# Attention into experts: exp's low parts moved from VectorE to GpSimd, with a new plan of times

## The chip, the cores and the metric

The kernel runs on one core of one Trainium2 chip. Its engines work side by side and meet at semaphores: TensorE (PE: matmuls and transposes, results to PSUM; PEld: its weight loads), VectorE (DVE), ScalarE (ACT), GpSimd (POOL, which does not read PSUM here) and SyncE (SP, whose queue issues all DMAs). The metric is device time in microseconds of one launch, as the median of several runs.

## The reference

```python
# q, k, v: (2, 8, 1152, 64) fp32
q_pool = q.reshape(B, H, S // 2, 2, D).mean(axis=3)          # 576 queries a head
scores = scale * q_pool @ k.transpose(0, 1, 3, 2)
attn = exp(scores - scores.max(-1, keepdims=True))
attn = attn / (attn.sum(-1, keepdims=True) + 1e-09)
x = (attn @ v) -> (1152, 512)
for e in range(4):                                            # w1 (4,512,1024), w2 (4,1024,512)
    out += p[:, e:e+1] * (relu(x @ w1[e]) @ w2[e])
a, b = out @ mw1, out @ mw2                                   # float64 weights
return ((a * b) @ w3) @ w_out
```

## The kernel before

Sixteen heads are worked in eight pairs (i = 0 to 7; s = 0, 1 is the head in the pair). To keep fp32's accuracy on fast matmuls, an operand is cut in a high part and a low part (value minus high part), and products of parts are summed.

For a pair, K is transposed on TensorE into bank tiles (`kt`, line 269) in two groups, six transposes and three; ScalarE copies the high part `kab` (line 272), VectorE the low part `kl` (line 275). GpSimd adds neighbouring queries (`pool_q`, lines 240 and 243), TensorE transposes them (`qt`, line 323), ScalarE writes the high part `qh` and rows 0 to 63 of QZ (lines 332, 333), VectorE the low part `ql` (line 326), and GpSimd rows 64 to 127 of QZ (line 329) in pieces of 512 and 64 columns. Row maxima come from cheaper matmuls (`mp`, line 381), five blocks for head 0 and four for head 1, each a two-bank and a one-bank tile (tags `w0`, `w1`, one buffer each) that VectorE reduces (`mx`, line 384). The maxima of a head (`mf`) are transposed (`mr`, line 416, also `w1`), cut (`mh` on ScalarE, `ml` on VectorE, line 424) and laid into Q2 by four small DMAs (`place`). DMAs (`plan_spread`) lay the parts of K and Q into K1, K2, Q1, Q2.

A head's scores come in nine chunks of 128 keys (`s`, line 535: four matmuls into one of two double banks). ScalarE writes the exp in fp32 (`pf`, line 545). Its upper 16 bits are the high part `pht`; the low part `plt` is `pf` minus that. GpSimd makes it (line 556) for chunks not in `LO_DVE`; for chunk 2 of head 0 and chunks 5 and 7 of head 1 ScalarE makes the exp a second time in the bank (`again`, line 549) and VectorE subtracts from there (line 554), so that the bank is held until then. V's parts are `v_hi` (line 510, ScalarE) and `v_lo` (line 514, VectorE). The attention product (`av`, lines 577 and 579) takes 135 small matmuls a head, ordered by five query blocks, then nine chunks, then three products; its first 27 therefore read all nine chunks. It is spread over the following half, with one accumulator bank, and `out_of` normalises it on VectorE (lines 583 to 595, `x` and `XT`).

All of this is written as an agenda: each step is entered with a time by `at(t, f)`, where one unit is about one chunk, and the steps are emitted in the order of their times. Nothing waits for a time: it only sets each engine's order of instructions. A pair has 18 units. The constants at the file's head are those times: `EX` to exp, `LO` and `LOV` to the low parts, `KT`, `KH`, `KL_` for K, `QT`, `QH_`, `QL_` for Q, `MX0`, `MX1` for maxima, `TURNS` for `mr`, `mh`, `ml` and `place`, `AV0`, `AVN` and `AVW` for start, length and density of the attention product.

The first expert's start is woven into the last pair: its weights (`WT`), the scale of x (`plan_rows`: `cm`, `cxt`, `ca`, `cxs`, `cx`, at `CX`), four transposes of x (`XA`, `XS`, `XC`, line 775 and lines 789, 794) which use a pool of three banks (`one_bank`) together with the spread of the weight maxima (`ws`, line 656, whose `bounds` run on VectorE at lines 445 to 449), two hidden tiles in four pieces each (`UA`, `US`) and two output tiles (`DT`, `DS`).

Of the kernel before, what the change touches and what calls it, by code (L numbers as in the profile page):

```python
# [9 lines left out]

TURN = 1.03
TURNS = (1.03, 1.23, 1.43, 1.93)
TURN0 = (0.05, 0.45, 0.55, 0.65)
KH = 0.79
KL_ = 0.32
QH_ = 0.05
QL_ = 1.2
M0 = 0.35
M1 = 0.01
M2 = 0.49  # L20
LO_DVE = ((2,), (5, 7))
EX = 0.44
EX2 = 0.6
LO = 0.9
LOV = 0.82
AV0 = 1.14
AVN = 7.68
AVW = ((0.8, 0.1, 0.85, 0.28, 1.25, 0.44, 0.55, 2.95), (1.0, 1.5, 0.42, 2.08, 1.5, 0.5, 0.62, 1.25))
VH = 0.35
VL = 2.06  # L30
VL0 = -5.21
VR = 5.67
VE = 0.9
V1 = (5.5, 1.4)
VL1 = 7.8
QZ1 = 0.25
VLZ = 2.7
K0 = 1.2
Q0 = 0.51
L0 = (5.7, 5.8)  # L40
LV2 = 15.6
PQ = 2.57
PQS = 0.3
SH = -5.85
XR = 136.9
CX = 128
CXT = (0, 0.3, 0.35, 1.2, 1.25)
LK1 = -10
LQ1 = -10
# [9 lines left out]
FIRST = (0.71, 1.14, 2.3, 3.1)  # L59
NEAR = 0.0  # L60
LATER = 0
KT = (3.05, 3.05)
QT = 4.84
MX0 = (7.0, 8.1, 9.9, 11.82, 13.01)
MXF = (7.3, 8.3, 10, 11.72, 13.01)
MX1 = (14, 16, 17.2, 18.92)
ME = -0.03
SW = 130
W1 = 134
WT = ((123.5, 129.6, 130.6, 132.7, 138.5, 133.3, 133.5, 135.6, 135.8), (2, 8.5))  # L70
WN = (1, 4, 5, 3, 0)
WN2 = (1, 4, 4, 3, 0)
WS = 6
XA = 0.2
XS = 1.1
XC = (0.75, 1.1)
UA = 136.6
US = 2
DT = (140.6, 143.8)
OUT = 0.1  # L80
XB = 147
DS = 1.1
TICKS = ((), (), (), (0, 1), (), (2,), (0, 4, 13), (2, 9), (), (0, 2, 10), (2, 8, 9), (14,), (0, 10), (2,), (2, 6, 14), (2, 4, 7), (0, 1))
FT = ((7,), (5,), (3,), (4,), (7,), (3,), (), (4,))
GT = ((0, 2), (2,), (0, 1, 2), (0, 2), (0, 1), (0, 1), (), (0,))
# [1 line left out]
W3T = 7  # L87
MX = 7
STAGED = 4
EV = 1  # L90

F32 = mybir.dt.float32
F32R = mybir.dt.float32r
# [18 lines left out]
def tile_kernel(ctx: ExitStack, tc: tile.TileContext, q, k, v, dp, w1, w2, mw1, mw2, mw3, mwo, out):  # L112
    nc = tc.nc
# [11 lines left out]
    NPAIR = B * H // 2  # L125
# [9 lines left out]
    f32 = lambda ap: ap.bitcast(F32)  # L135
# [55 lines left out]
    QZ = k_p.tile([P, 2 * T], F32R, name="QZ")  # L191
# [7 lines left out]
    KAB, KL, QH, QL = {}, {}, {}, {}  # L199
# [32 lines left out]
    def at(t, f, *args):  # L232
        agenda.append((t, len(agenda), f, args))
# [18 lines left out]
    def plan_k(i, t):  # L252
# [7 lines left out]
        for g in range(2):  # L260
# [54 lines left out]
    def plan_q(i, t, tv):  # L315
        st = {}

        def pe():
            QH[i] = kq_p.tile([P, T], F32R, tag="qh", name=f"qh{i}")
            QL[i] = kq_p.tile([P, T], F32R, tag="ql", bufs=1, name=f"ql{i}")  # L320
            ps = st[0] = work(0, f"qt{i}").rearrange("p n c -> p (n c)")
            for j in range(NB + 1):
                nc.tensor.transpose(ps[:, j * P : (j + 1) * P], QP[:, j], ident)  # L323

        def lo():
            nc.vector.tensor_tensor(out=QL[i], in0=st[0][:, :T], in1=f32(QH[i]), op=ALU.subtract)

        def one(lo, hi, to):
            nc.gpsimd.tensor_copy(QZ[64:128, to : to + hi - lo], f32(QH[i][64:128, lo:hi]))

        at(t, pe)
        at(tv, lambda: nc.scalar.copy(out=QH[i], in_=st[0][:, :T]))
        at(tv + 0.02, lambda: nc.scalar.copy(out=QZ[0:64, :T], in_=st[0][0:64, :T]))
        at(tv + QL_, lo)
        tz = tv + (QZ1 if i == 1 else 0.6)
        at(tz, one, 0, NB * P, T + TL)
        at(tz, one, NB * P, T, T)

# [20 lines left out]
    def plan_max(i, s, times):  # L359
# [29 lines left out]
        for t, j in zip(times, blocks):  # L389
            at(t + NEAR, pe, j, 0)  # L390
            at(t + M0, reduce, j, 0)
            at(t + (M1 if i == 0 else 2 * NEAR), pe, j, 1)
# [128 lines left out]
    def plan_scores(i, s, t):  # L521
        for c in range(NC):
            st = {}

            def pe(c=c, st=st):
                if c == 0:
                    if i + s:
                        pft[i, s] = ph_p.tile([P, NC, T], F32, tag="pf", name=f"pf{i}_{s}")
                    pht[i, s] = pft[i, s].bitcast(BF16).rearrange("p c (t w) -> p c t w", w=2)[:, :, :, 1]
                    plt[i, s] = ph_p.tile([P, NC, T], F16, tag="pl", name=f"pl{i}_{s}")  # L530
                ps = st["s"] = ps_s.tile([P, 2, 512], F32, tag="s", name=f"s{i}_{s}_{c}")
                cs = slice(c * P, (c + 1) * P)
                for a, b, first in ((K1, Q1, True), (K2, Q2, False)):
                    for n in range(2):
                        mm(  # L535
                            ps[:, n, :HALF], a[s][:, cs], b[s][:, n * HALF : (n + 1) * HALF],
                            start=first, stop=not first,
                        )

            two = lambda ap: ap.rearrange("p (n t) -> p n t", n=2)  # L540

            on_dve = c in LO_DVE[s]

            def whole(c=c, st=st):
                nc.scalar.activation(out=two(pft[i, s][:, c, :]), in_=st["s"][:, :, :HALF], func=AF.Exp, scale=SCORE)  # L545

            def again(c=c, st=st):
                x = st["s"][:, :, :HALF]
                nc.scalar.activation(out=x, in_=x, func=AF.Exp, scale=SCORE)

            def lo(c=c, st=st, on_dve=on_dve):
                o, f, h = plt[i, s][:, c, :], pft[i, s][:, c, :], pht[i, s][:, c, :]
                if on_dve:
                    nc.vector.tensor_tensor(out=two(o), in0=st["s"][:, :, :HALF], in1=two(h), op=ALU.subtract)  # L554
                else:
                    nc.gpsimd.tensor_tensor(out=o, in0=f, in1=h, op=ALU.subtract)  # L556

            at(t + c, pe)
            at(t + c + EX, whole)
            if on_dve:  # L560
                at(t + c + EX2, again)
            at(t + c + (LOV if on_dve else LO), lo)

    def plan_av(i, s, t, span):
        b, h = PAIRS[i]
        xd = slice((h + s) * D, (h + s + 1) * D)
        xo = X[b][:, :, xd]
        st = {}

        def one(j, c, n):  # L570
            if (j, c, n) == (0, 0, 0):
                st["t"] = ps_a.tile([P, NB + 1, D + 1], F32, tag="a", name=f"av{i}_{s}")
            o = j * P if j < NB else T - P
            p = (pht, pht, plt)[n][i, s][:, c, o : o + P]
            t = st["t"]
            if n == 1:
                mm(t[:, j, 0:D], p, vt[s][:, c, 0:D], start=False, stop=False)  # L577
            else:
                mm(t[:, j, :], p, vt[s][:, c, D:], start=(c == 0 and n == 0), stop=(c == NC - 1 and n == 2))  # L579

        def out_of():
            dn = tiny.tile([P, NB + 1], F32, tag="dn", name=f"dn{i}_{s}")
            nc.vector.tensor_scalar(
                out=dn, in0=st["t"][:, :, D], scalar1=PS * EPS, scalar2=vs[i][:, s : s + 1],
                op0=ALU.add, op1=ALU.mult,
            )
            nc.vector.reciprocal(out=dn, in_=dn)
            n = NB if b else NB + 1
            nc.vector.tensor_tensor(
                out=xo[:, :n], in0=st["t"][:, :n, :D], in1=dn[:, :n].unsqueeze(2).to_broadcast([P, n, D]), op=ALU.mult  # L590
            )
            if b:
                r = slice(64, 128)
                nc.vector.tensor_scalar(  # L594
                    out=XT[r, xd], in0=st["t"][r, NB, :D], scalar1=dn[r, NB:], scalar2=None, op0=ALU.mult
                )

        todo = [(j, c, n) for j in range(NB + 1) for c in range(NC) for n in range(3)]

        share = AVW[s] if span == AVN else (1,) * 8  # L600
        ends = [sum(share[:n]) / sum(share) for n in range(9)]
        for k, x in enumerate(todo):
            y = k / len(todo)
            n = max(m for m in range(8) if ends[m] <= y)
            at(t + span * (n + (y - ends[n]) / (ends[n + 1] - ends[n])) / 8, one, *x)
        at(t + span + OUT, out_of)


# [240 lines left out]
    with tc.manual_schedule():  # L849
# [15 lines left out]
        for b in range(B):  # L865
            nc.sync.dma_start(
                out=pr_raw[:, b * NB : (b + 1) * NB, :],
                in_=dp[b * T : b * T + NB * P].rearrange("(p j) e -> p j e", j=NB),
# [33 lines left out]
        for i in range(NPAIR):  # L902
            nx = i + 1 < NPAIR
            t = 18 * i
# [8 lines left out]
            if nx:  # L913
# [3 lines left out]
                u = t + (LATER if i == 0 else 0)  # L917
# [110 lines left out]
    with tc.manual_schedule():  # L1028
# [182 lines left out]
        for t, (pe, add) in enumerate(down_tiles(last_task, bank)):  # L1211
# [10 lines left out]
            if t in (4, 6, 8):  # L1222
                lo, hi = {4: (0, 4), 6: (4, 6), 8: (6, 9)}[t]
# [115 lines left out]
```

## Time and profile before

| | us |
|---|---|
| runs | 823.51, 821.10, 821.26; median 821.26 |
| profiled execution | 819.96 |
| its span, first to last instruction | 818.2 |
| PE busy | 797.2 (97%) |
| DVE busy | 609.6 (75%) |
| ACT busy | 405.1 (50%) |
| POOL busy | 274.3 (34%), nearly all before 260 us |

Attention is the first third of the span. In times shown as 121.77 the span's start is zero. A matmul's record is longer than its share of TensorE, because matmuls overlap: the step from one start to the next is what TensorE spends.

### The profile page before, as it was taken

How to read it: one execution, taken by the hardware profiler on the slowest of the kernel's cores; microseconds unless marked ns; L12 is line 12 of the kernel's file. 1: busy time of each engine (PE TensorE's matmuls, PEld its weight loads, DVE VectorE, ACT ScalarE, POOL GpSimd, SP SyncE). 2: the span in 40 equal slices, each digit the busy share in tenths (PEclk: the TensorE clock that was granted, in tenths of full speed). 3: DMA queues.
4: the chain of work that ended last, by engine and by line, in shares of the span. 5: the costliest groups of instructions: out<-in, count | busy, mean ns of one | idle time of the engine just before them, and what ended most of it. 6: DMA issues, size and time to landing. Idle time of an engine off the chain costs nothing.

```text
span 818.2 us, 15685 instructions
## 1 busy us (share of the span) xinstructions
PE 797.2 (97%) x6301; PEld 523.9 (64%) x6301; DVE 609.6 (75%) x1086; ACT 405.1 (50%) x735; POOL 274.3 (34%) x264
## 2 busy tenths in 40 slices
PE   8799999999999999999999999999999999999998
PEld 7688888888877555555555555555554446556787
DVE  6888889888885666779978999988788877772000
ACT  2565666566573543334445466636564545553111
POOL 5667766676661000001101124303331323442100
PEclk9999999999999999999999999999999999999999
DMA  8866756684630121123323332321357752300011
GB/s 185 219 142 165 186 135 151 154 182 105 162 80 2 52 103 52 52 78 103 108 74 103 104 103 78 103 77 52 80 143 139 176 127 75 97 3 1 14 52 51
DMA packets 85976, 83.28 MB, mean 102 GB/s; under 512 B 49624, under 2 KB 67408, under 8 KB 85904
## 3 DMA queue, kind: packets, MB, share of 16 engines
q1 hardware_dynamic: 85904, 82.29, 38.9%
q8 instruction: 49, 0.80, 0.4%
q14 instruction: 23, 0.19, 0.1%
HBM read 51.92 MB, written 2.36 MB: 66 GB/s over the span
## 4 chain that ended last, share of the span: by engine, by line
PE 86%; DVE 9%; DMA 2%; issue 1%; ACT 1%; SPq 1%; POOL 0%; DVEq 0%; ACTq 0%; POOLq 0%
PE up L705 23%; PE dn L745 22%; PE gt L1277 11%; PE s L535 7%; PE o L1293 6%; PE wf L1246 5%; PE mp L381 4%; PE av L579 4%; DVE mx L384 4%; PE av L577 2%; DVE pl L554 1%; DMA rk<-in_k 1%; DVE vt L514 1%; DMA rw<-in_moe_w 1%; PE qt L323 1%
## 5 line engine op out<-in xcount | busy, mean ns | idle before, releaser
L745 PE MATMUL dn<-w,h 128*128 128x512 f16 x840 | 183.9, 379 | 0.0
L556 POOL TENSOR_TENSOR pl<-pf 128x576 f16<-128x576 f32 x120 | 140.4, 1186 | 67.8 <-ACT pf L545 67.7
L705 PEld LDWEIGHTS <-w 128*128 128x128 f16 x1152 | 111.6, 98 | 76.0 <-DVE w L676 0.8
L745 PEld LDWEIGHTS <-h 128*128 128x128 f16 x840 | 81.5, 98 | 95.7
L545 ACT ACTIVATE pf<-s 128x576 f32<-128x576 f32 x144 | 93.2, 649 | 55.9 <-PE s L535 55.4
L535 PE MATMUL s<-Q,K 128*128 128x288 f32 x576 | 110.4, 314 | 2.9 <-ACT pf L545 1.7
L384 DVE TENSOR_REDUCE mx<-mp 128x1 f32<-128x768 f32 (+1 forms) x144 | 101.8, 751 | 13.4 <-PE mp L381 11.9
L705 PE MATMUL up<-xB,w 128*128 128x320 f16 x768 | 109.9, 299 | 0.5 <-DVE xB L794 0.5
L844 POOL TENSOR_TENSOR wo<-wo,cv_a 128x512 f32<-128x512 f32 x20 | 25.8, 1293 | 226.6 <-DVE wo L841 128.8
L711 ACT ACTIVATE up<-up 128x320 f32<-128x320 f32 (+1 forms) x96 | 45.8, 477 | 112.9 <-PE up L705 91.7
L705 PE MATMUL up<-xA,w 128*128 128x512 f16 x384 | 89.0, 379 | 0.3 <-DVE w L676 0.3
L535 PEld LDWEIGHTS s<-Q,K 128*128 128x128 f32 x576 | 83.9, 191 | 4.9 <-ACT pf L545 2.1
L579 PE MATMUL av<-vt,pf 128*128 128x65 f16 x720 | 83.1, 194 | 1.6 <-DVE XT L594 1.5
L579 PE MATMUL av<-vt,pl 128*128 128x65 f16 x720 | 83.2, 195 | 0.0
L577 PE MATMUL av<-vt,pf 128*128 128x64 f16 x720 | 82.2, 193 | 0.0
L716 DVE TENSOR_TENSOR h<-up,h 128x320 f16<-128x320 f32 (+1 forms) x94 | 50.1, 550 | 42.9 <-ACT h L712 42.5
L1277 PEld LDWEIGHTS <-mw 128*128 128x128 f16 x576 | 55.9, 98 | 36.8
L579 PEld LDWEIGHTS <-pf 128*128 128x128 bf16 x720 | 66.9, 99 | 8.3 <-DVE XT L594 2.8
L579 PEld LDWEIGHTS <-pl 128*128 128x128 f16 x720 | 67.0, 97 | 4.6 <-issue 1.1
L577 PEld LDWEIGHTS <-pf 128*128 128x128 bf16 x720 | 67.1, 98 | 3.9 <-issue 1.1
L381 PE MATMUL mp<-kab,QZ 128*128 128x384 f32 x216 | 57.8, 374 | 1.3 <-DVE mx L384 1.0
L759 DVE SCALAR_TENSOR_TENSOR x2B<-dn,sh,x2B 128x512 f32<-128x512 f32 x75 | 52.9, 743 | 4.7 <-PE dn L745 4.0
(183 smaller groups left out, 1200.4 us busy)
## 6 DMA issues: line engine op xcount, KB each, us to landing
rw<-in_moe_w SPq DMA_DIRECT2D x64, 512.0 KB
K<-kab SPq DMA_DIRECT2D x32, 288.0 KB
rk<-in_k SPq DMA_DIRECT2D x16, 288.0 KB
rv<-in_v SPq DMA_DIRECT2D x8, 576.0 KB
Q<-qh SPq DMA_DIRECT2D x32, 144.0 KB
K<-kl SPq DMA_DIRECT2D x16, 288.0 KB
rq<-in_q SPq DMA_DIRECT2D x8, 512.0 KB
rw<-in_moe_w_out SPq DMA_DIRECT2D x8, 512.0 KB
```

The lines of the kernel that those rows point to most:

```text
L381: mm(ps[:, n, :PC], QZ[:, o : o + P], KAB[i][:, sl], start=True, stop=True)
L384: nc.vector.tensor_reduce(out=mx[i, s][:, j, g : g + 1], in_=st.pop((j, g))[:, :, :PC], axis=AX.XY, op=ALU.max)
L535: mm(ps[:, n, :HALF], a[s][:, cs], b[s][:, n * HALF : (n + 1) * HALF], start=first, stop=not first,)
L545: nc.scalar.activation(out=two(pft[i, s][:, c, :]), in_=st["s"][:, :, :HALF], func=AF.Exp, scale=SCORE)
L556: nc.gpsimd.tensor_tensor(out=o, in0=f, in1=h, op=ALU.subtract)
L577: mm(t[:, j, 0:D], p, vt[s][:, c, 0:D], start=False, stop=False)
L579: mm(t[:, j, :], p, vt[s][:, c, D:], start=(c == 0 and n == 0), stop=(c == NC - 1 and n == 2))
L705: mm(p, w[:, a, c, fc * P : (fc + 1) * P], x[b][:, c, lo - o : hi - o], start=(c == 0 and a == b), stop=(c == KD - 1 and a == 1),)
L716: nc.vector.tensor_tensor(out=hl[:, fc, lo:hi], in0=st["p"], in1=hh[:, fc, lo:hi], op=ALU.subtract)
L745: mm(p, hid[n][a][:, fc, t * P : (t + 1) * P], w[:, b, fc, :], start=(fc == 0 and a == b), stop=(fc == 1 and a == 1),)
L759: nc.vector.scalar_tensor_tensor(out=acc, in0=st["p"], scalar=share, in1=acc, op0=ALU.mult, op1=ALU.add)
L1277: mm(p, mws[n][:, a, m * KD + c], x[:, b * KD + c, lo - o : hi - o], start=(c == 0 and a == b), stop=(c == KD - 1 and a == 1),)
```

## The change

`LO_DVE` becomes empty, so in pairs 0 to 6 GpSimd makes all eighteen low parts; in the last pair `LASTD` names chunk 4 of head 0 and chunks 0 and 7 of head 1 for VectorE. The upper 512 columns of QZ's lower half are copied by ScalarE from PSUM. Chunks get times of their own (`SPOS`, not in pair 0), the attention matmuls' times are rounded up to steps of 0.02 (`AVS`), and most other times are new.

```diff
-TURNS = (1.03, 1.23, 1.43, 1.93)
+TURNS = (1.08, 1.18, 2.08, 2.53)
-KH = 0.79
-KL_ = 0.32
-QH_ = 0.05
-QL_ = 1.2
-M0 = 0.35
+KH = 0.49
+KL_ = 0.62
+QH_ = 1.1
+QL_ = 0.25
+M0 = 0.4
-LO_DVE = ((2,), (5, 7))
-EX = 0.44
-EX2 = 0.6
-LO = 0.9
-LOV = 0.82
-AV0 = 1.14
-AVN = 7.68
-AVW = ((0.8, 0.1, 0.85, 0.28, 1.25, 0.44, 0.55, 2.95), (1.0, 1.5, 0.42, 2.08, 1.5, 0.5, 0.62, 1.25))
-VH = 0.35
-VL = 2.06
-VL0 = -5.21
-VR = 5.67
-VE = 0.9
+LO_DVE = ((), ())
+LASTD = ((4,), (0, 7))
+LOL = 0.85
+EX = 0.79
+EX2 = 0.85
+LO = 2.45
+LOV = 1.15
+AV0 = 1.49
+AVN = 7.48
+AVW = ((0.64, 0.05, 1.06, 0.45, 1.0, 0.14, 0.2, 2.36), (0.8, 1.47, 1.71, 2.49, 0.72, 0.32, 0.55, 1.54))
+VH = 0.8
+VL = 2.36
+VL0 = -5.71
+VR = 4.82
+VE = 0.2
...
-PQ = 2.57
-PQS = 0.3
+PQ = 0.52
+PQS = 0.65
-XR = 136.9
-CX = 128
+XR = 138.35
+CX = 128.8
-KT = (3.05, 3.05)
-QT = 4.84
-MX0 = (7.0, 8.1, 9.9, 11.82, 13.01)
+KT = (3.05, 3.5)
+QT = 4.54
+MX0 = (7.0, 8.1, 9.35, 12.27, 13.06)
+SPOS = ((0, 0.8, 2.1, 3, 4.4, 5, 6.2, 7, 7.9), (0.1, 1, 2.1, 3, 4, 5, 6, 7, 7.65))
+AVS = 0.02
+AVP = 2.35
-MX1 = (14, 16, 17.2, 18.92)
-ME = -0.03
-SW = 130
-W1 = 134
+MX1 = (14.0, 16.2, 17.25, 18.82)
+ME = 0.12
+SW = 130.8
+W1 = 133.8
...
-XA = 0.2
-XS = 1.1
-XC = (0.75, 1.1)
-UA = 136.6
-US = 2
-DT = (140.6, 143.8)
-OUT = 0.1
+XA = 0.35
+XS = 0.55
+XC = (0.9, 1.1)
+UA = 135.5
+US = 2.1
+DT = (140.8, 144.1)
+OUT = 0.35
...
         def one(lo, hi, to):
-            nc.gpsimd.tensor_copy(QZ[64:128, to : to + hi - lo], f32(QH[i][64:128, lo:hi]))
+            if lo:
+                nc.gpsimd.tensor_copy(QZ[64:128, to : to + hi - lo], f32(QH[i][64:128, lo:hi]))
+            else:
+                nc.scalar.copy(out=QZ[64:128, to : to + hi - lo], in_=st[0][64:128, lo:hi])
...
-            on_dve = c in LO_DVE[s]
+            on_dve = c in (LO_DVE[s] if i < NPAIR - 1 else LASTD[s])
...
-            at(t + c, pe)
-            at(t + c + EX, whole)
+            u = t + (SPOS[s][c] if i else c)
+            at(u, pe)
+            at(u + EX, whole)
             if on_dve:
-                at(t + c + EX2, again)
-            at(t + c + (LOV if on_dve else LO), lo)
+                at(u + EX2, again)
+            at(u + (LOV if on_dve else LO if i < NPAIR - 1 else LOL), lo)
...
-            at(t + span * (n + (y - ends[n]) / (ends[n + 1] - ends[n])) / 8, one, *x)
+            u = t + span * (n + (y - ends[n]) / (ends[n + 1] - ends[n])) / 8
+            if span == AVN:
+                u = math.ceil((u - AVP) / AVS) * AVS + AVP
+            at(u, one, *x)
```

## Rows read from the trace of the kernel before

**Rows 1.** Page: the chain that ended last, share of the span by engine.
```profile
PE 86%; DVE 9%; DMA 2%; issue 1%; ACT 1%; SPq 1%; POOL 0%; DVEq 0%; ACTq 0%; POOLq 0%
```
**Rows 2.** Stretches: length, busy time of PE, PEld, DVE, ACT, POOL, clock, DMA share, GB/s.
```profile
18.80:32.79 13.99, 9.82 (x56) 7.44 (x56) 11.17 (x23) 7.64 (x15) 7.05 (x9) 1.00 0.87 204
32.79:36.20 3.41, 3.34 (x12) 3.23 (x13) 2.80 (x6) 1.27 (x4) 3.25 (x3) 0.50 1.11 298
121.77:150.16 28.39, 27.55 (x392) 24.33 (x389) 24.81 (x42) 17.36 (x29) 20.01 (x21) 1.00 0.68 158
```
**Rows 3.** Waits of weight loads, 36.63 to 221.2: who for whom, us, times, longest.
```profile
PEld mp L381 <- DVE mx L384: 5.9, 32, 0.3
PEld kt L269 <- DVE ml L424: 5.8, 6, 1.0
...
PEld s L535 <- DVE pl L554: 1.7, 7, 0.2
```
**Rows 4.** VectorE in order of time, 138 to 142.9: start, us, instruction.
```profile
138.75 2.12 DVE L514 SCALAR_TENSOR_TENSOR vt<-rv,vs,vt 128x576 f16<-128x576 f32 x1
140.79 0.74 DVE L554 TENSOR_TENSOR pl<-s,pf 128x576 f16<-128x576 f32 x1
141.46 0.27 DVE L424 TENSOR_TENSOR ml<-mr,mh 5x128 f32<-5x128 f32 x1
```
**Rows 5.** Groups of ScalarE, 121.77 to 150.16: busy us, mean ns, idle before.
```profile
L549 ACT ACTIVATE s<-s 128x576 f32<-128x576 f32 x3 | 1.9, 647 | 0.0
...
L333 ACT CAST QZ<-qt 64x576 fp32r<-64x576 f32 x1 | 0.6, 631 | 0.0
```
**Rows 6.** Groups of GpSimd, 121.77 to 150.16.
```profile
L556 POOL TENSOR_TENSOR pl<-pf 128x576 f16<-128x576 f32 x16 | 18.6, 1178 | 8.1 <-ACT pf L545 8.1
```
**Rows 7.** Order of time, 120 to 165, matmuls.
```profile
121.72 0.19 PE L577 MATMUL av<-vt,pf 128*128 128x64 f16 x1
121.75 0.19 PE L579 MATMUL av<-vt,pl 128*128 128x65 f16 x1
...
121.77 0.79 PE L535 MATMUL s<-Q,K 128*128 128x288 f32 x4
...
123.00 0.69 PE L535 MATMUL s<-Q,K 128*128 128x288 f32 x4
```
**Rows 8.** Order of time, 133.5 to 136.3: last `place` DMA, next pair's first chunk.
```profile
133.63 0.53 SPq L430 DMA_DIRECT2D Q<-ml  x1
...
136.00 0.51 PE L535 MATMUL s<-Q,K 128*128 128x288 f32 x2
```
**Rows 9.** VectorE in order of time, 228 to 236.
```profile
229.32 0.80 DVE L514 SCALAR_TENSOR_TENSOR vt<-rv,vs,vt 128x576 f16<-128x576 f32 x1
...
232.36 1.03 DVE L448 TENSOR_SCALAR wab<-wab 128x2 f32<-128x2 f32 x1
...
233.50 0.73 DVE L794 SCALAR_TENSOR_TENSOR xA<-xt,cx,xA 128x512 f16<-128x512 f32 x1
```
**Rows 10.** Line 556, whole span: ns shortest, median, longest.
```profile
L556 POOL TENSOR_TENSOR pl<-pf x120: 1139/1147/2104, 24.3 to 252.4; 128x576 f16<-128x576 f32 x120
```
**Rows 11.** Waits of matmuls, 25 to 33.5.
```profile
PE mr L416 <- DVE mf L401: 1.4, 1, 1.4
PE qt L323 <- DVE kl L275: 1.0, 1, 1.0
PE s L535 <- ACT pf L545: 0.7, 1, 0.7
PE vp L461 <- DVE vm L457: 0.4, 1, 0.4
```
**Rows 12.** Waits of matmuls, 221.2 to 262.
```profile
PE av L579 <- DVE XT L594: 1.3, 2, 0.7
PE s L535 <- ACT pf L545: 1.0, 2, 0.6
PE s L535 <- DVE cx L497: 0.4, 1, 0.4
PE cxt L482 <- DVE cm L476: 0.3, 1, 0.3
```

More of the change, by code (lines that the diff above doesn't have):

```diff
@@ L11 @@
 TURN = 1.03
-TURNS = (1.03, 1.23, 1.43, 1.93)
+TURNS = (1.08, 1.18, 2.08, 2.53)
 TURN0 = (0.05, 0.45, 0.55, 0.65)
-KH = 0.79
-KL_ = 0.32
-QH_ = 0.05
-QL_ = 1.2
-M0 = 0.35
+KH = 0.49
[3 more added lines that the diff above has]
+M0 = 0.4
 M1 = 0.01
 M2 = 0.49
-LO_DVE = ((2,), (5, 7))
-EX = 0.44
-EX2 = 0.6
-LO = 0.9
-LOV = 0.82
-AV0 = 1.14
-AVN = 7.68
-AVW = ((0.8, 0.1, 0.85, 0.28, 1.25, 0.44, 0.55, 2.95), (1.0, 1.5, 0.42, 2.08, 1.5, 0.5, 0.62, 1.25))
-VH = 0.35
-VL = 2.06
-VL0 = -5.21
-VR = 5.67
-VE = 0.9
+LO_DVE = ((), ())
[13 more added lines that the diff above has]
+VE = 0.2
 V1 = (5.5, 1.4)
 VL1 = 7.8
-QZ1 = 0.25
-VLZ = 2.7
+QZ0 = 0.25
+QZ1 = 0.1
+VLZ = 2.55
 K0 = 1.2
@@ L61 @@
 LATER = 0
-KT = (3.05, 3.05)
-QT = 4.84
-MX0 = (7.0, 8.1, 9.9, 11.82, 13.01)
-MXF = (7.3, 8.3, 10, 11.72, 13.01)
-MX1 = (14, 16, 17.2, 18.92)
-ME = -0.03
-SW = 130
-W1 = 134
-WT = ((123.5, 129.6, 130.6, 132.7, 138.5, 133.3, 133.5, 135.6, 135.8), (2, 8.5))
+KT = (3.05, 3.5)
[4 more added lines that the diff above has]
+AVP = 2.35
+MXF = (7.3, 8.3, 10, 11.72, 13.01)
+MX1 = (14.0, 16.2, 17.25, 18.82)
+ME = 0.12
+SW = 130.8
+W1 = 133.8
+WT = ((123.5, 129.6, 130.6, 132.7, 138.5, 133.3, 133.5, 135.6, 135.8), (2, 8.8))
 WN = (1, 4, 5, 3, 0)
@@ L73 @@
 WS = 6
-XA = 0.2
-XS = 1.1
-XC = (0.75, 1.1)
-UA = 136.6
-US = 2
-DT = (140.6, 143.8)
-OUT = 0.1
-XB = 147
-DS = 1.1
+XA = 0.35
[5 more added lines that the diff above has]
+OUT = 0.35
+XB = 148.6
+DS = 1.3
 TICKS = ((), (), (), (0, 1), (), (2,), (0, 4, 13), (2, 9), (), (0, 2, 10), (2, 8, 9), (14,), (0, 10), (2,), (2, 6, 14), (2, 4, 7), (0, 1))
@@ L89 @@
 STAGED = 4
-EV = 1
+EV = 1.3
 F32 = mybir.dt.float32
@@ L334, in plan_q @@
         at(tv + QL_, lo)
-        tz = tv + (QZ1 if i == 1 else 0.6)
+        tz = tv + (QZ0 if i == 1 else QZ1)
         at(tz, one, 0, NB * P, T + TL)
```

## The prediction

> **What bounds the kernel now.** I read the chain of waits first. TensorE carries 86% of it and VectorE 9% [rows 1], so a microsecond is won only where TensorE stands still. The change touches the attention stage and its seam to the experts, up to about 262 us; what follows has the same work in the same order. So I took the busy time of stretches. One pair of heads lasts 28.39 us (121.77 to 150.16) with VectorE busy 24.81, ScalarE 17.36 and GpSimd 20.01 [rows 2]: no helper is full, but VectorE at 87% is late at places. The stretch 32.79 to 36.20 stands out: TensorE was granted half its clock there, after 13.99 us in which it was busy only 9.82 [rows 2].
>
> Then TensorE's waits. From 36.63 to 221.2 its weight loads waited 5.9 us in 32 waits for a row maximum, 5.8 us in 6 waits (0.97 each) on line 269 for `ml`, and 1.7 us in 7 waits on line 535 for the VectorE subtraction of line 554 [rows 3]. The 0.97 comes once a pair: the second group of K transposes needs the bank that the turned maxima `mr` still hold until `ml` has read it. On VectorE `ml` stood behind 2.12 us of `vt` (line 514) and 0.74 of line 554 [rows 4].
>
> **The change part by part.** *Low parts to GpSimd.* In seven pairs three chunks each lose a second exp (0.647 on ScalarE [rows 5]) and a VectorE subtraction (0.74 [rows 4]) and get a GpSimd subtraction (1.178 [rows 6]). Per pair ScalarE loses 1.9, VectorE 2.2, and GpSimd gains 3.5. The upper 512 columns of QZ go from GpSimd to ScalarE; that copy is not in the trace, and lies between zero and the 0.631 of the 576-column copy beside it [rows 5]; I take 0.6, the nearest row. GpSimd then has 20.0 + 3.5 - 0.6 = 22.9 us of a pair of about 27.5, ScalarE 16.1, VectorE 22.6. The extra copy sits ahead of one exp; the score chunk that needs this exp's bank comes two chunks and some 24 attention matmuls later, about 2 x 0.7 + 24 x 0.03 = 2.1 us [rows 7], against 0.6 + 0.65. I cost it at nothing; without that cover it is 0.6 in 7 pairs, 4.2 us.
>
> *What this takes off TensorE.* The 1.7 us of waits for line 554 go: the bank is now free after one exp. The K transposes are helped twice: 0.74 is gone ahead of `ml`, and the second group is asked for 0.45 plan units later with ten attention matmuls in between, 0.3 us. 0.74 + 0.3 covers the 0.97, but `mr` moves behind a score chunk and `vt` stays directly ahead, so I leave 0.2: 6 x 0.77 = 4.6 us gained (bounds: nothing, 5.8). For the maxima I take 1.0 of the 5.9 (0 to 5.9): their spacing changes both ways, and a wait of 0.18 is partly the weight load that could not run ahead.
>
> *What is added on TensorE.* A score chunk directly behind attention matmuls takes 0.79, behind a maxima matmul 0.69 [rows 7]: a switch costs 0.10. Laid out by their times, a pair has 24 such switches where it had 21: 3 x 7 x 0.10 = 2.1 at most; two of the three stand before short transposes, and I take 1.5. Middle pairs: -4.6 - 1.7 - 1.0 + 1.5 = -5.8 us.
>
> *Moved steps with no cost.* `place` (four DMAs) comes half a plan unit later in the SP queue, past nothing but its own wait; K and Q loads swap. The last of the four `ml`/`mh` DMAs is issued at 133.63 and takes 0.53, and the next pair's first chunk, their reader, starts at 136.00 [rows 8]: 1.8 us of cover for issue and landing, of which the change takes about 0.3. The Q pooling on GpSimd goes behind two low parts (2.4 us), with about 5 us until its transpose. The vector `vp` matmul is asked for one chunk earlier than the reduction behind it may be done; it waited 0.4 for that in the first pair [rows 11], so 0 to 0.4 a pair; I take 0, since `ml` and `kl` ahead of it start earlier too.
>
> *Port.* Line 514 shows two lengths, 0.80 [rows 9] and 2.12 [rows 4], and a GpSimd low part of 1.147 median reached 2.104 [rows 10]. The 2.12 stand in the middle pairs, where line 514 meets GpSimd at work already, so I add nothing. [...]
>
> *First pair.* In it TensorE waits 1.4 us for `mf`, 1.0 for `kl` and 0.7 for an exp [rows 11]. `mf` comes 0.75 earlier without line 554. The first K transposes now come before `mr`, so they run inside that wait; `kl` for six transposes is asked separately, ahead of the reduction. The exp that held a bank no longer stands behind the Q copies. I take 1.8 of the 3.1. The half clock I leave in; if it went, 3.41 us would become 1.7.
>
> *Last pair and first expert tiles.* TensorE's waits there: 1.3 for `XT` (the normalised output), 1.0 for exp, 0.4 and 0.3 around the scale chain `cx`, `cm`, 3.0 together [rows 12]. In the new order an expert piece stands between chunks 0 and 1 of the second head, both down pieces stand ahead of the last attention head, and `cxt` comes behind `mr`: all four waits should go. New ones come. The spread `cxs` follows `cxt` after 23 matmuls (0.7 us) while its chain has five small VectorE operations, each at most about the 0.27 of `ml` [rows 4], 1.35 in all: 0 to 0.65, and I take 0.4. And the fourth x transpose follows the weight spread `ws` at once; it needs the bank of the second, whose VectorE half stands behind the weight scales: 1.03 for the slowest of these and 0.73 for the half itself [rows 9]. That is between 0.73 and about 2.2; I take 1.8. Net -3.0 + 0.4 + 1.8 = -0.8 us.
>
> **Sum.** -5.8 - 1.8 - 0.8 = -8.4 us. The profiled execution took 819.96 us, a span of 818.2 and 1.76 around it; it becomes 811.6. The median of three runs is 821.26, 1.3 above the profiled one; from it the forecast is 812.9.
>
> **Rivals.**
> B, the port gives the gain back. Each of two `vt` operations a pair stays at 2.12 or grows by one more low part (1.15), `ml` is late again and the K wait stays: the 4.6 and the 1.0 are lost, and middle pairs are -1.7 + 1.5 = -0.2. With the first and last pair at half of my figures, -1.3: 819.8. For it: line 514 was 2.12 where GpSimd worked without a break, and GpSimd will do so more. Against: line 554 is gone from that queue in any case.
>
> C, slower: GpSimd becomes the bound. The attention matmuls read all nine low parts of a head in their first 27, so a late one stops TensorE. GpSimd's 22.9 us leave 5.5 of a pair of 28.39, 0.305 for each of 18 low parts: it decides once their mean passes 1.178 + 0.305 = 1.48 us, which lies between the median and the longest [rows 10]. At 1.53 a pair lasts 18 x 0.05 = 0.9 longer: 7 x 0.9 = 6.3 us, 827.6. Against: two collisions a pair of the longest kind, 0.96 each, add only 0.11 to the mean.
>
> D, the seam eats more. The new waits at `cxs` and the fourth transpose take 0.4 + 2.2, the low part of chunk 4 on VectorE holds the bank of chunk 6 for its 0.74, a third of the old 3.0 comes back, and TensorE's clock falls as it fell after the waits of the first pair: 3.41 us at half clock, 1.7 lost. The seam is then -3.0 + 2.6 + 0.7 + 1.0 + 1.7 = +3.0 in place of -0.8: 816.7.
>
> E, the stage is freed further: maxima waits halve (2.0 more), and the half clock of the first pair goes (1.7): 809.2.
>
> **How the numbers follow.** Chances: forecast 0.46, E 0.14, D 0.13, B 0.16, C 0.11. A measurement tells 0.3% (2.5 us) from no change. The forecast, E and D are faster; B is mostly the same, split 0.03, 0.10, 0.03; C slower 0.10, same 0.01. Together faster 0.76, same 0.11, slower 0.13. The forecast's own range is 809 to 817; 8 in 10 reach from 806 (E with all K waits gone) to 821.5 (B with a new wait of 0.25 a pair), leaving C and a little of B and E out.
>
> **What would show it.** Pairs of about 27.5 us in place of 28.39, and no wait of line 269 above 0.3 each; no line 554 before 200 us, and 22 to 23.5 us of GpSimd a pair; a transpose of the fourth x block that waits 1 to 2 us for VectorE; the half-clock stretch still near 33 us. It is wrong if attention matmuls wait for `pl`, if line 514 has a mean over 2.1, or if a middle pair is longer than 28.2 us.

## The result, and the profile after

The changed kernel takes 813.03 us (median of 4 runs, 812.85 to 813.24) against 821.64 of the kernel before beside it: 0.9891 of its time, with an interval of 0.9874 to 0.9908. The forecast was 812.9. The profiled execution took 812.85 us with a span of 811.1, which is 7.1 less than the 819.96 and 818.2 of before.

TensorE's work did not get smaller (6301 matmuls in both kernels), it waits less. From the page, the chain that ended last, by engine [rows 1]:

```profile
PE 86%; DVE 10%; DMA 1%; ACT 1%; issue 1%; SPq 0%; ACTq 0%
```

Busy time of stretches: length, PE, PEld, DVE, ACT, POOL, clock, DMA share, GB/s [rows 2]. The second is where TensorE ran at half clock before; the third is one pair of heads.

```profile
18.97:32.80 13.83, 10.59 (x60) 8.01 (x60) 11.23 (x25) 7.14 (x14) 7.82 (x10) 1.00 0.91 202
32.80:36.20 3.40, 2.95 (x16) 2.34 (x17) 2.58 (x4) 2.07 (x5) 3.40 (x4) 1.00 0.97 238
132.74:160.35 27.61, 27.40 (x393) 24.43 (x389) 22.39 (x39) 16.06 (x27) 23.27 (x23) 1.00 0.72 162
```

A pair lasts 27.61 us in place of 28.39, with TensorE busy all but 0.21 of it. GpSimd has 23.27 us and VectorE 22.39 (22.9 and 22.6 were expected), and the half clock is gone in this execution.

Waits of weight loads from 35.47 to 215.5, all groups [rows 3]:

```profile
PEld mp L390 <- DVE mx L393: 4.2, 19, 1.1
PEld L589 <- issue: 2.2, 14, 0.2
PEld mp L390 <- DVE ql L332: 2.2, 6, 0.4
PEld L587 <- issue: 1.9, 12, 0.2
PEld L589 <- DVE XT L604: 0.5, 2, 0.3
```

The 5.8 us of the K transposes for `ml` and the 1.7 for the old VectorE subtraction have no row any more, the maxima fell from 5.9 to 4.2, and a new row has come: maxima matmuls wait 0.37 a pair for `ql`. Why the first went is seen on VectorE and GpSimd in order of time (start, us, instruction) [rows 4]:

```profile
135.96 0.15 DVE L410 TENSOR_REDUCE mf<-mx 128x1 f32<-128x2 f32 x1
136.03 0.81 DVE L523 SCALAR_TENSOR_TENSOR vt<-rv,vs,vt 128x576 f16<-128x576 f32 x1
137.06 0.28 DVE L433 TENSOR_TENSOR ml<-mr,mh 5x128 f32<-5x128 f32 x1 [0.22 <-ACT mh L429]
...
141.66 1.04 DVE L457 TENSOR_SCALAR vs<-vs 128x2 f32<-128x2 f32 x1
142.74 0.17 DVE L458 RECIPROCAL vs<-vs 128x2 f32<-128x2 f32 x1
142.85 0.76 DVE L332 TENSOR_TENSOR ql<-qt,qh 128x576 fp32r<-128x576 f32 x1
```
```profile
134.33 1.15 POOL L565 TENSOR_TENSOR pl<-pf 128x576 f16<-128x576 f32 x1 [1.44 <-ACT pf L554]
135.44 1.98 POOL L246 TENSOR_TENSOR QP<-rq 128x256 f32<-128x256 f32 x2
137.39 1.14 POOL L565 TENSOR_TENSOR pl<-pf 128x576 f16<-128x576 f32 x1
...
141.54 2.38 POOL L565 TENSOR_TENSOR pl<-pf 128x576 f16<-128x576 f32 x2
```

`vt` took 0.81 us here where it took 2.12: it came in between the two pooling adds of line 246, and `ml` now waits for ScalarE, not for `vt`. The new wait for `ql` starts at line 457: two columns of four bytes took 1.04 us, because a low part had begun on GpSimd 0.12 earlier (shown below, one column at a time). With GpSimd idle, at 19.2, the same operation took 0.17.

Low parts on GpSimd in that pair [rows 6] and the new copy on ScalarE (busy us, mean ns, idle before):

```profile
L565 POOL TENSOR_TENSOR pl<-pf 128x576 f16<-128x576 f32 x19 | 21.9, 1174 | 4.3 <-ACT pf L554 4.1
```
```profile
L338 ACT CAST QZ<-qt 64x512 fp32r<-64x512 f32 x1 | 0.6, 583 | 0.0
```

Waits of matmuls in the first pair, 18.97 to 35.47 [rows 11]:

```profile
PE mp L390 <- DVE mx L393: 1.0, 4, 0.4
PE mp L390 <- ACT QZ L338: 1.0, 1, 1.0
PE kt L275 <- DVE ml L433: 0.7, 1, 0.7
PE qt L329 <- DVE kl L281: 0.4, 1, 0.4
PE vp L470 <- DVE kl L281: 0.4, 1, 0.4
PE kt L275 <- DVE mx L393: 0.2, 1, 0.2
```

And from 215.5 to 262, the seam to the experts [rows 12]:

```profile
PE cxs L503 <- DVE cxd L497: 1.3, 1, 1.3
PE up L718 <- DVE xB L807: 0.5, 1, 0.5
PE xt L788 <- DVE xB L807: 0.3, 1, 0.3
PE xt L788 <- DVE wab L454: 0.2, 1, 0.2
```

A half of a pair begins with its first score chunk. Measured from one such start to the next, in the profiled executions of this case:

| kernel | first pair | half with K transposes | other half | median us | ratio to before |
|---|---|---|---|---|---|
| before | 17.85 + 14.19 | 14.17 | 14.23 | 821.3 to 822.0 | 1 |
| changed | 16.50 + 14.49 | 13.95 | 13.63 | 813.03 | 0.9891 [0.9874, 0.9908] |
| new plan, old low parts | 16.70 + 14.92 | 13.96 | 14.09 | 817.42 | 0.9942 [0.993, 0.9954] |
| before, low parts alone | 17.00 + 14.47 | 17.2 (15.7 once) | 13.93 | 834.85 | 1.0159 [1.014, 1.0177] |
| before, pooling alone | 17.30 + 14.77 | 13.75 | 14.23 | 819.33 | 0.9969 [0.9959, 0.9979] |
| before, low parts and pooling | 16.78 + 14.48 | 13.36 | 13.94 | 814.63 | 0.9925 [0.99, 0.995] |
| changed, old pooling | 16.53 + 14.50 | 15.06 | 13.64 | 821.01 | 1.0001 [0.9989, 1.0012] |
| changed, one column | 16.42 + 14.46 | 13.56 | 13.62 | 810.73 | 0.9861 [0.9848, 0.9875] |
| one column, QZ from SBUF | 15.94 + 13.90 | 13.60 | 13.62 | 809.49 | 0.9857 [0.9842, 0.9871] |
| one column, QZ on GpSimd | 15.82 + 14.50 | 13.38 | 13.63 | 808.28 | 0.9834 [0.982, 0.9848] |

Of the 7.1 us, twelve middle halves have 4.8, the first pair and its start 0.9, and the last pair with all that follows 1.4. That last figure has two parts: the last attention matmul starts 2.1 us sooner after the start of its half (21.68 in place of 23.83), and 0.7 is lost again far behind, in expert work that the change does not touch. From the 401st to the 801st matmul of the output tiles (line 758) the changed kernel takes 169.1 us, the kernel before 168.4, and the others of the table 169.0 to 170.3.

### The profile page after: what moved, and what is told of

Read it like the earlier page. It is cut to its first block, busy times and chain, and to the rows that moved or that the text cites. A ratio compares the mean times of both kernels' runs of the same rounds, so it can differ in the third digit from the quotient of the medians.

```text
span 811.1 us, 15625 instructions
## 1 busy us (share of the span) xinstructions
PE 794.8 (98%) x6301; PEld 522.8 (64%) x6301; DVE 593.3 (73%) x1065; ACT 396.0 (49%) x722; POOL 295.7 (36%) x277
## 4 chain that ended last, share of the span: by engine, by line
PE 86%; DVE 10%; DMA 1%; ACT 1%; issue 1%; SPq 0%; ACTq 0%
PE dn L758 21%; PE up L718 21%; PE gt L1290 12%; PE s L544 8%; PE o L1306 6%; PE wf L1259 5%; PE av L589 5%; PE mp L390 5%; DVE mx L393 3%; PE av L587 2%; DVE vt L523 1%; PE kt L275 1%; DVE vs L457 1%; DVE ql L332 1%; DMA rk<-in_k 1%; DMA rw<-in_moe_w 1%
## 5 line engine op out<-in xcount | busy, mean ns | idle before, releaser
L565 POOL TENSOR_TENSOR pl<-pf 128x576 f16<-128x576 f32 x141 | 162.7, 1175 | 48.7 <-ACT pf L554 47.5
L589 PE MATMUL av<-vt,pf 128*128 128x65 f16 x720 | 85.0, 194 | 0.1
L544 PEld LDWEIGHTS s<-Q,K 128*128 128x128 f32 x576 | 82.0, 189 | 2.4 <-issue 0.6
```

The lines of the kernel that those rows point to most:

```text
L544: mm(ps[:, n, :HALF], a[s][:, cs], b[s][:, n * HALF : (n + 1) * HALF], start=first, stop=not first,)
```

## The experiments

**The new plan without the moved low parts.** The changed kernel with the old choice of chunks in pairs 0 to 6.

```diff
-LO_DVE = ((), ())
+LO_DVE = ((2,), (5, 7))
```


> The new plan of times with the old share of low parts (chunk 2 of head 0, chunks 5 and 7 of head 1 again on VectorE with a second exp, pairs 0 to 6). Theory 1, the gain comes from work taken off VectorE and off the score banks: the 0.74 us ahead of the cut maxima and the bank waits come back, 5 to 7 us slower than the changed kernel, near 818 to 820. Theory 2, the gain comes from the order (K transposes in two steps, expert pieces between chunks): within 2 us of the changed kernel, 813 to 815.

817.42 us, between the ranges of the two theories. By the ratios the plan alone is worth 4.8 of a gain of 9.0, the moved low parts under it the other 4.2. They show where VectorE used to subtract from the bank in head 1: 14.09 against 13.63. The halves with K transposes take 13.96 here as in the changed kernel, and the weight loads of the K transposes wait 0.3 us in all from 36.17 to 217, although a subtraction again stands ahead of `ml`:

```profile
138.51 0.81 DVE L523 SCALAR_TENSOR_TENSOR vt<-rv,vs,vt 128x576 f16<-128x576 f32 x1
139.25 0.76 DVE L563 TENSOR_TENSOR pl<-s,pf 128x576 f16<-128x576 f32 x1
139.93 0.27 DVE L433 TENSOR_TENSOR ml<-mr,mh 5x128 f32<-5x128 f32 x1
```

So in the new plan that wait went without the moved low parts, with `vt` at 0.81.

**The moved low parts without the new plan.**

```diff
-            on_dve = c in LO_DVE[s]
+            on_dve = i == NPAIR - 1 and c in LO_DVE[s]
```


> The old plan of times with all low parts of pairs 0 to 6 on GpSimd, and nothing else. Theory 1: most of the gain of the middle pairs and half of that of the first pair without a new plan: waits of line 269 for the cut maxima fall from 0.97 to about 0.2 and the waits for line 554 go; 4 to 7 us faster than before, 815 to 818. Theory 2: less than 2 us faster, 820 to 822, because the old times put something else in the way.

834.85 us: 13 slower. The part that I took for the source of the gain costs more, alone, than the whole change brings. The waits of weight loads from 36 to 235, then VectorE and GpSimd at one of the places:

```profile
PEld kt L269 <- DVE ml L424: 15.1, 6, 2.5
```
```profile
84.87 0.15 DVE L401 TENSOR_REDUCE mf<-mx 128x1 f32<-128x2 f32 x1
84.93 4.32 DVE L514 SCALAR_TENSOR_TENSOR vt<-rv,vs,vt 128x576 f16<-128x576 f32 x1
89.18 0.27 DVE L424 TENSOR_TENSOR ml<-mr,mh 5x128 f32<-5x128 f32 x1
```
```profile
84.87 0.45 POOL L243 TENSOR_TENSOR QP<-rq 64x128 f32<-64x128 f32 x1
85.29 3.35 POOL L556 TENSOR_TENSOR pl<-pf 128x576 f16<-128x576 f32 x3
```

`vt` began 0.06 us behind a pooling add and ended 0.61 after the last of three low parts that GpSimd ran directly behind it: 4.32 us for an operation that took 0.81 in the changed kernel. Both its inputs (`rv`, `vt`) lie in SBUF, as GpSimd's do. `ml` stands behind it, and the K transposes wait for `ml`. This is rival B's mechanism at twice the size that I gave it: 2.2 us more than the 2.12 of before, where I priced 1.15. Where a K wait was that long, TensorE was granted half its clock for 3.41 us behind it in five of the six pairs of the profiled execution, as in the first row here; the mean clock of the pair around it was 0.95 (columns of rows 2):

```profile
89.56:92.97 3.41, 3.41 (x37) 3.20 (x38) 2.57 (x3) 1.13 (x2) 0.31 (x1) 0.50 0.17 37
84.90:116.00 31.10, 28.83 (x388) 25.68 (x386) 24.89 (x39) 15.79 (x26) 23.24 (x24) 0.95 0.62 143
```

Wait and clock together are the 3.1 us by which those halves grew: the wait is 2.5 in place of 0.97, and the one half that kept its clock is 1.5 shorter (15.7). The trace shows that `vt` was kept out through four instructions of GpSimd (3.70 us), and not by what.

So which other edit of the change keeps `vt` out of this? The candidate was the Q pooling, whose add stood ahead of those low parts.

**Before, with the low parts and the pooling's new times.** To the edit above:

```diff
-PQ = 2.57
-PQS = 0.3
+PQ = 0.52
+PQS = 0.65
```


> The kernel before, with GpSimd making all low parts of pairs 0 to 6, and with one more thing of the change: the Q pooling on GpSimd at its new times (PQ 0.52, PQS 0.65). Theory (the 13 us lost by the low parts alone are VectorE's vt, which is kept out of work as long as GpSimd runs instructions one directly behind the other, and the pooling adds are what made GpSimd late there): the 64-row pooling add no longer stands ahead of three waiting low parts, vt drops from up to 4.33 us to below 2.2, the halves with K transposes go from about 17.2 us back to 14.4 or less, total 814 to 820. Rival 1 (the low parts overload GpSimd under the old times wherever the pooling stands): vt stays above 3 us once a pair, total 830 to 836. Rival 2 (the K transposes' times, not vt, make the wait): vt short, but the wait of the K transposes for ml stays above 1 us a pair, total 821 to 829.

814.63 us. Two constants took back 19 us (by the ratios). `vt` at the same place, and GpSimd:

```profile
80.62 1.71 DVE L514 SCALAR_TENSOR_TENSOR vt<-rv,vs,vt 128x576 f16<-128x576 f32 x1
82.25 0.27 DVE L424 TENSOR_TENSOR ml<-mr,mh 5x128 f32<-5x128 f32 x1
```
```profile
79.46 2.25 POOL L556 TENSOR_TENSOR pl<-pf 128x576 f16<-128x576 f32 x2 [1.59 <-ACT pf L545]
81.67 1.24 POOL L240 TENSOR_TENSOR QP<-rq 128x256 f32<-128x256 f32 x1
82.88 1.14 POOL L556 TENSOR_TENSOR pl<-pf 128x576 f16<-128x576 f32 x1
```

`vt` now meets one low part and gets in ahead of the pooling add, which is the one that waits (1.24 us; with the low parts alone two of these adds took 1.43 together, at 82.13). The wait of the K transposes is gone, and the halves with them, 13.36 us, are shorter than in the changed kernel. The theory's figure for `vt` (below 2.2) and total held; both rivals fell.

**The changed kernel with the pooling's old times.** The same edit the other way round.

> The changed kernel with the Q pooling on GpSimd back at its old times (PQ 2.57, PQS 0.3) and nothing else. Theory (the pooling's place decides whether vt meets an unbroken run of GpSimd): vt above 2 us in middle pairs again, ml and the K transposes late, halves with K transposes above 14.5 us in place of 13.95, total 818 to 832. Rival (the new plan of turns and K transposes has enough room, and the pooling's time matters little): vt may be long, but TensorE does not wait for it, total 812 to 815.

821.01 us: the whole gain is gone. Waits of weight loads from 36 to 220, and `vt` beside GpSimd:

```profile
PEld kt L275 <- DVE ml L433: 7.5, 6, 1.3
```
```profile
81.87 2.60 DVE L523 SCALAR_TENSOR_TENSOR vt<-rv,vs,vt 128x576 f16<-128x576 f32 x1
84.40 0.27 DVE L433 TENSOR_TENSOR ml<-mr,mh 5x128 f32<-5x128 f32 x1
```
```profile
80.50 3.35 POOL L565 TENSOR_TENSOR pl<-pf 128x576 f16<-128x576 f32 x3
84.69 1.15 POOL L565 TENSOR_TENSOR pl<-pf 128x576 f16<-128x576 f32 x1 [0.84 <-ACT pf L554]
```

**The pooling's new times alone, in the kernel before.**

> The kernel before with the Q pooling on GpSimd at its new times (PQ 0.52, PQS 0.65) and nothing else: what the move of the pooling is worth without the low parts. Theory (two separate terms: the pooling shortens only the run of GpSimd that vt meets, and the low parts take their subtraction of 0.74 out of VectorE's queue ahead of ml): vt in the halves with K transposes 1.7 to 1.8 instead of 2.12, the wait of the K transposes for ml 0.5 to 0.7 instead of 0.97, total 818 to 820.5. Rival 1 (the pooling's place was the whole gain of the kernel with low parts and pooling, 7 us): 813.5 to 816. Rival 2 (without the low parts the pooling's time does nothing): 821 to 822.5.

819.33 us, the theory's range. `vt` fell from 2.12 to 1.70 and the wait of the K transposes from 5.8 to 3.3 us in 6. With it the four corners are there: pooling alone -2.6, low parts alone +13, both -6.2 (all by their ratios). The moved low parts are worth -3.6 behind a moved pooling and +13 without it.

What `vt` took follows in each kernel from what GpSimd ran, by the records of both near the same place of a pair:

| kernel | GpSimd while `vt` stood there | ends after `vt`'s start | `vt` us |
|---|---|---|---|
| before | add, low part | 1.50 | 2.12 |
| pooling alone; low parts and pooling | rest of a low part | 1.09 | 1.71 |
| low parts alone | add, three low parts | 3.70 | 4.32 |
| changed, old pooling | rest of a low part, low part | 1.99 | 2.60 |
| changed | rest of an add | 0.14 | 0.81 |

In each row `vt` ends 0.61 to 0.67 us after the GpSimd instruction that kept it out.

**The bounds and `cxd` one column at a time.** The same arithmetic in more and smaller operations.

```diff
-        nc.vector.tensor_scalar(out=up, in0=up, scalar1=top, scalar2=low, op0=ALU.mult, op1=ALU.max)
+        for n in range(up.shape[-1]):
+            x = up[:, n : n + 1]
+            nc.vector.tensor_scalar(out=x, in0=x, scalar1=top, scalar2=low, op0=ALU.mult, op1=ALU.max)
...
-            nc.vector.tensor_scalar(
-                out=cxd[0:B], in0=ident[0:B, 0:B], scalar1=a[:, 1:2], scalar2=None, op0=ALU.mult
-            )
+            for n in range(B):
+                nc.vector.tensor_scalar(
+                    out=cxd[0:B, n : n + 1], in0=ident[0:B, n : n + 1], scalar1=a[:, 1:2], scalar2=None, op0=ALU.mult
+                )
```


> The changed kernel, with the small two-column VectorE operations (the scaling of the power of two in bounds and of cxd) written one column at a time, the same numbers in twice the instructions. Theory, such an operation from SBUF to SBUF with more than one column waits for GpSimd's running instruction, with one column it does not: the 1.04 us of the middle pairs and the 1.07 us of cxd become two of 0.15 to 0.2 each; the wait of cxs falls from 1.3 to about 0.6, ql comes 0.7 earlier in each pair and the maxima matmuls no longer wait for it: 2 to 3 us faster than the changed kernel, 810 to 811. Rival, the length has another cause (the place in the queue, the operand): one of the two columns takes the 1.0 us again, same time or up to 1 us slower.

810.73 us. VectorE at the place of the 1.04 us, and GpSimd beside it:

```profile
140.47 0.21 DVE L459 TENSOR_SCALAR vs<-vs 128x1 f32<-128x1 f32 x2
140.72 0.17 DVE L460 RECIPROCAL vs<-vs 128x2 f32<-128x2 f32 x1
140.85 0.76 DVE L332 TENSOR_TENSOR ql<-qt,qh 128x576 fp32r<-128x576 f32 x1
```
```profile
140.35 2.37 POOL L568 TENSOR_TENSOR pl<-pf 128x576 f16<-128x576 f32 x2
```

Two instructions take a fifth of the one, with GpSimd as busy as before. The waits for `ql` went (13.95 to 13.56), and that for `cxd` fell from 1.3 to 0.6, as the theory said. The 1.04 us and the 0.21 each stood beside a low part that had begun 0.12 earlier. The number of columns is not all of it: the reciprocal behind them, 128x2 too, took 0.17 beside the same low part. What makes the scaling of two columns wait is not shown by any run.

**The QZ copy read from SBUF.** `st[0]` is the bank that `ql` also reads.

```diff
-                nc.scalar.copy(out=QZ[64:128, to : to + hi - lo], in_=st[0][64:128, lo:hi])
+                nc.scalar.copy(out=QZ[64:128, to : to + hi - lo], in_=f32(QH[i][64:128, lo:hi]))
```


> The changed kernel, but ScalarE copies the upper part of QZ from qh in SBUF instead of from the PSUM bank of the transposed Q. Theory, the copy costs TensorE time because it and the VectorE subtraction for ql take turns at one PSUM tile: ql no longer waits for the copy nor the copy for ql, the 1.0 us wait of the first pair's maxima matmul for the QZ copy goes and the 0.37 a pair of maxima matmuls for ql shrinks by half, 1.5 to 2.5 us faster than the changed kernel, 810.5 to 811.5. Rival, ql is late because of VectorE's own queue and the copy because of ScalarE's: the same within 0.5 us, 812.5 to 813.5.

812.38 us (ratio 0.9883, interval 0.9868 to 0.9898): not to be told from the changed kernel by its time, so the 1.5 to 2.5 us of the theory did not come. Its trace shows the first pair's wait for this copy gone and 1.26 us won there, of which a start 0.55 later hides a part. The middle pairs are unchanged.

**`mr` ahead of the K transposes in the first pair.**

```diff
-        e = times[-1] + 1 + ME
+        e = times[-1] + 1 + (ME if i else -0.03)
```


> The changed kernel with the turned maxima of the first pair asked for before its K transposes, as in the kernel before (in the first pair only). Theory (the half clock near 33 us went because the K transposes now run inside TensorE's wait for mf): the wait of mr for mf comes back with about 1.4 us and a stretch of 3.41 us at half clock with it, first pair 1.4 to 3 us longer, total 814.5 to 816.5. Rival (the half clock went because of something else, the missing second exps or the earlier QZ copy): the wait comes back, the clock stays at 1.00, total 813 to 814.5.

814.19 us (ratio 0.9913, interval 0.9898 to 0.9927). The wait for `mf` is back with 1.0 us, and the clock stays at 1.00 (columns as above):

```profile
30.00:33.00 3.00, 1.69 (x14) 1.43 (x13) 2.67 (x3) 2.57 (x5) 0.60 (x3) 1.00 0.65 163
33.00:37.00 4.00, 2.84 (x15) 2.00 (x15) 3.04 (x7) 2.46 (x5) 4.00 (x4) 1.00 0.82 176
```

So that wait alone does not bring the half clock. In the kernel before with the pooling alone, whose waits are nearly those of before, the same stretch is at 1.00 too, and from 215 to 262, at 1.00 before, the mean clock is 0.96 instead. The clock also differs between executions of one kernel: the mean over the span is 0.996 to 1.000 in the four of this one, and 1.000 in 13 of the 39 executions of the kernel before that were timed beside the experiments (lowest 0.995). What brings it stays open, and one profiled execution at 1.00 does not show that the change removed it.

**Both mends together, and then QZ back on GpSimd.**

> The changed kernel with the two edits that gained by themselves: the QZ copy on ScalarE read from QH in SBUF, so that it does not come behind ql by the bank, and the multi-column tensor_scalar operations of the bounds and of cxd written one column at a time. Theory (the two remove different waits, the first pair's 1.0 for the copy and the 0.37 a pair for ql with 0.7 at the seam): they add up, 0.65 and 2.3 off 813.0, so 809 to 810.8. Rival (both remove the same stall of ql, or the first pair's gain is given back at its start, which began 0.5 later in that run): no better than the one-column kernel alone, 810.7 or more.

809.49 us, 0.9857: they remove different waits, but the step past one column alone is within the intervals. The weight load of a score chunk still waits 0.2 us for an exp once a pair (1.0 in six). The second edit puts the copy where it was in the kernel before:

```diff
-            if lo:
-                nc.gpsimd.tensor_copy(QZ[64:128, to : to + hi - lo], f32(QH[i][64:128, lo:hi]))
-            else:
-                nc.scalar.copy(out=QZ[64:128, to : to + hi - lo], in_=f32(QH[i][64:128, lo:hi]))
+            nc.gpsimd.tensor_copy(QZ[64:128, to : to + hi - lo], f32(QH[i][64:128, lo:hi]))
```


> The changed kernel with the bounds and cxd one column at a time, and the upper 512 columns of QZ copied by GpSimd as in the kernel before instead of ScalarE. Theory (the copy on ScalarE delays one exp a pair, whose bank a score chunk then waits 0.2 for): that wait goes, the halves with K transposes fall from 13.60 to about 13.4 us, the first pair keeps its 15.9, total 807.5 to 809. Rival (half a microsecond more of GpSimd work ahead of low parts and vt costs as much or more): 809.5 to 812.

808.28 us, 0.9834: the fastest kernel here, 0.6% under the changed one. The halves with K transposes went from 13.60 to 13.38, as expected. A pair of it, in the columns of rows 2:

```profile
130.93:157.97 27.04, 26.95 (x388) 24.33 (x387) 21.56 (x40) 15.46 (x26) 23.76 (x23) 1.00 0.72 166
```

GpSimd does 23.76 us of 27.04, and TensorE is idle for only 0.09.

**Old times for head 0 in that kernel.** K, Q, V, the turns, exp, the low parts, head 0's chunks and its attention product get the times of before (`TURNS`, `KH`, `KL_`, `QH_`, `QL_`, `KT`, `QT`, `MX0`, `EX`, `LO`, `AV0`, `AVN` and others), head 1's chunks, maxima and the density of its attention product, the pooling and the seam keep the new ones.

> The kernel of the run before this one, with the times of the kernel before for K, Q, V, the turns, exp and head 0 of a pair, and the new ones for the pooling, head 1 and the seam. Theory (the new times of the halves with K transposes gained nothing: the kernel with the low parts and the pooling alone has them at 13.35 us, against 13.60 with new times and one-column operations): 13.35 and 13.62 us for the two halves of a pair, total 806 to 808.5. Rival (the two halves are bound to each other by what is left over at the turn, and the mixture opens new waits): 809.5 or more.

812.61 us (ratio 0.9893, interval 0.9875 to 0.9911): the rival. The halves with K transposes take 13.38 to 13.60, no better than with the new times, and all but one of the others 14.02 in place of 13.63. `EX`, `LO`, `AV0` and `AVN` serve head 1 as well, so it did not keep all its new times, and 14.02 lies near the 13.94 that it takes in the old plan with moved low parts. Which of these times costs it stays open.

## Why the prediction was right, and where its reasons were not

**The sum.** It said -8.4 on the profiled execution, which gave -7.1 there and -8.6 by the medians. By stretches: middle pairs -5.8 said, -4.8 (twelve halves) and +0.1 (the thirteenth) measured; first pair -1.8 said, -0.9 measured; seam -0.8 said, -2.1 measured up to the last attention matmul, with +0.7 of scatter far behind it. So the 0.1 us between 812.9 and 813.03 is luck: every stretch was off, in both directions, and the profiled execution gained 1.3 less than was said. Of the signs, the lengths of pairs and the GpSimd time came as named; the wait of the fourth x transpose and the half clock near 33 us did not.

**Middle pairs.** Right: the 5.8 for `ml` and the 1.7 for line 554 went, and the maxima gave 1.7 where I took 1.0. Missing: the wait for `ql`, 2.2 in six pairs. I had put it at nothing without naming it; its cause is line 457, 0.56 before and 1.04 after. The QZ copy "at nothing" was wrong as well: two kernels with one-column operations that differ in the copy alone are 0.2 apart in each half with K transposes, 1.2 in six. The step from chunk 6 to chunk 7 of head 0 shows it in the changed kernel itself: 0.92 us (from 132.74), and 0.75 in the fastest kernel, so the cover of 2.1 us for 1.25 did not hold for all chunks. -5.8 - 1.7 - 1.7 + 2.2 + 1.2 is -5.8; 1.0 us of loss remains, of the size of the 1.5 for switches, but no run shows that term by itself: the kernel before with low parts and pooling, with fewer switches, has the same 13.36 us as the fastest kernel's 13.38.

**The step that failed** is "Moved steps with no cost", on the pooling: "The Q pooling on GpSimd goes behind two low parts (2.4 us), with about 5 us until its transpose." I asked whether its reader would be late, and it is not. I did not ask what it moves on GpSimd for VectorE: with the low parts moved, its place decides over 19 us in the old plan and 9 in the new, by the ratios. By my reckoning the K wait went by 0.74 + 0.3 against 0.97. In truth `vt` itself gave 1.3 in the changed kernel, and the plan alone lost the wait with the subtraction still ahead of `ml`. Had the pooling not moved, the wait would have been 1.3 a pair in the new plan (`vt` 2.60) and 2.5 in the old one (`vt` 4.32). In the old plan the 0.74 did count: with the pooling moved, 0.55 a pair was left with the subtraction there, and nothing without it.

**Port.** "The 2.12 stand in the middle pairs, so I add nothing" came out right for the changed kernel (`vt` 0.91 in the median, 1.66 at most, from 36 to 230) and for a wrong reason. 2.12 was no upper end: it was one add and one low part, and with two low parts more it was 4.32, 1.1 for each. Nor had line 514 two lengths: before, from 36 to 230, it took 0.80 to 2.12, with 1.43 to 1.45 in the second half of four pairs. Rival B was the mechanism to fear; its price of one more low part was half of what the low parts alone showed, and the half clock behind the wait was not in it. No run shows a port: what they show is that `vt` ended 0.61 to 0.67 us after the GpSimd instruction that kept it out.

**GpSimd as the bound (C)** did not come near: the mean low part stayed at 1.174 against a limit of 1.48, and no attention matmul waits for `pl`.

**First pair.** The waits for `mf` and exp went as said (2.1), that for `kl` fell by 0.6. New ones took most of it back: 1.0 for the QZ copy, which comes behind `ql` there and waits 0.83 for it at their shared bank, 0.9 at the K transposes, 0.2 more for maxima, and 0.30 in the pair's second half. The rows thus leave some 0.3 of gain, and the half clock that went should have added 1.7; 0.9 was measured, its start 0.2 later among it. The 1.7 looks too large: with the pooling alone the half clock was gone there too, and that half was only 0.55 shorter, with 0.5 more of waits for maxima; in the changed kernel TensorE is busy for 2.95 of the 3.40 us of rows 2. How much of the missing 1.1 this is stays open.

**Seam.** All four old waits went, 3.0. `cxs` waited 1.3 where I took 0.4: `cxd`, two columns from SBUF to SBUF, took 1.07 us beside GpSimd's low parts, where I had bounded each of the five operations by 0.27. Rows 9 held the warning: 1.03 for a two-column operation on the weights, which I used for the other wait only. The fourth x transpose waited 0.2, not 1.8: it waits for the reader of `ws` (line 454 here), so it had the bank of `ws` and not that of the second transpose. The two waits for `xB` are not new: the kernel before has them too, 0.5 and 0.3, behind 262. So the rows give -3.0 + 1.3 + 0.2 = -1.5 in place of -0.8, two errors of opposite sign; 0.6 of the 2.1 measured has no row.

## What to carry to other kernels

Before work is moved to GpSimd, list the VectorE operations of the kinds that grew beside it here (`vt` with its two SBUF inputs, 0.81 to 4.32 us, and the scaling of 128x2 in SBUF, 0.17 to 1.04), and ask what GpSimd runs without a break when each of them starts; what stands behind them on VectorE can pay for that whole run, as the K transposes did with 2.5 us a pair. Price a moved step by what it changes for its neighbours on its own engine, not by its reader's slack alone. And where a change has two parts, test them together as well as alone, for their effects need not add up: here -2.6 and +13 made -6.2.

## What the runs showed of the hardware that was not expected

With the low parts alone `vt` waited through several instructions of GpSimd: through an add and three low parts, 3.70 us. It is not always so long. The median `vt` of that kernel took 1.76 us; in the changed kernel, at 66.75 us, it was let in after one low part though another stood directly behind it (1.62 us), and ahead of a pooling add it came in at once in every middle pair (0.81 us, as beside an idle GpSimd at 224.19). What decides between two instructions of GpSimd stays open. And the scaling of 128x2 took 1.04 us beside GpSimd, where two of 128x1 took 0.21 together.
